# Attention backward on one core: the q rows on ScalarE's queue, more dK blocks ahead of the reciprocal, and an earlier start of V's work in the last turn

## The chip, the core and the metric

The kernel runs on one of the eight cores of a Trainium2 chip. A core has five engines with queues of their own: TensorE (PE, whose weight loads are listed as PEld), VectorE (DVE), ScalarE (ACT), GpSimd (POOL) and SyncE (SP). Sixteen DMA engines move data between HBM and SBUF; here nearly all transfers are issued from SP's queue, in order. An instruction waits on semaphores until what it needs is there, and whatever stands behind it on its queue waits with it. The metric is the device time in microseconds. Before the change it is 634.97 us (median of three runs, 634.79 to 635.12).

## The reference

There are 32 heads, one query row each (Sq = 1), 8192 keys and values of 128 numbers, all bf16. Forward output and three gradients are wanted:

```python
scores = einsum('bhqd,bhkd->bhqk', q, k) * 128 ** -0.5
attn = softmax(scores, axis=-1)
out = einsum('bhqk,bhkd->bhqd', attn, v)
# returned: out, dq, dk, dv for a given grad_out
```

With p the softmax row of a head and g its row of grad_out, dv is the outer product of p and g, dp = V g, ds = p (dp - sum(p dp)) / sqrt(128), dq = K^T ds and dk is the outer product of ds and q. K and V are 67 MB each. Each is read once, and dk and dv, of the same sizes, are written once: 268 MB in all.

## The kernel before

**Turns.** Two heads make one pair, and pair t is worked on in turn t, of 16 (HP = 16). A K or V tile of a pair is 4.19 MB, [128 partitions, 128 rows, 128 numbers]. K has three buffers, V two. The gradient overwrites its input in place: `outer(t, "p", r)` writes one eighth of dV over V, and `outer(t, "ds", r)` one eighth of dK over K (both L363, on DVE); `store` (L373, on SP) then sends the tile out. In turn t the kernel finishes pair t-1's dK ("old" work, called by `dk(a, b)` for blocks a to b-1, with the store behind the block that completes a part), computes the softmax and dV of pair t, and starts pair t+1's scores. A 17th pass of the loop does the last dK.

**Scores.** `k_block(t, c)`: DVE transposes an eighth of K (L197), PE multiplies it with the q columns (L205) into one PSUM bank. `s_back` transposes the result on DVE (L212), `s_top` and the head of `s_exp` find the maximum over the partitions with a PE transpose between (L217 to L227), ScalarE does the exponential (L230), and `s_sum` adds over partitions on PE (L235). `p_of` takes the reciprocal on DVE (L246), and ScalarE writes p four times (`p_rep`, L248) and puts it into a window (L241) for the contraction `contract(t, "p")` (PE, L341), which makes the forward output.

**V's part.** dP = V g wants V transposed. `v_bank(t, m)` transposes a sixteenth of it on PE, four matmuls into one of three PSUM tiles (L269), `v_copy` takes it to SBUF on ScalarE (L275); `v_part` is both. When four banks m = 4z to 4z+3 are copied, `v_scores(t, z)` multiplies them with grad_out's columns (PE, L286). In turns 3 to 14 (`wide(t)`, the loop's branch `blocks`) the second half of V goes by DVE transposes instead (`v_block`, L293, and `v_wide`, L303). Turns 0, 1, 2 and 15 have no such V blocks; turn 0 does all sixteen banks before the loop. `v_back` (L312, L315) transposes dP back on DVE, `ds_of` computes ds, `contract(t, "ds")` makes dq.

**Order.** It is written out by hand: within `tc.manual_schedule()` each engine runs its instructions in the order in which the program emits them. In turns 1, 2 and 15 that order is: dK blocks 0 to 2, banks 3 and 4, `s_back`, `s_top`, scores 0, banks 5 and 6, the exponential, banks 7 to 9 on PE, `s_sum`, copies 7 and 8, dK block 3, `p_of`, copy 9, scores 1, banks 10 and 11, the contraction, banks 12 and 13, scores 2, banks 14 and 15, scores 3, dK blocks 4 to 7, dV blocks 0 and 1, `v_back`, dV block 2, `ds_of`, `contract(t, "ds")`, and dV blocks 3 to 7. Banks 0 to 2 of pairs 1, 2 and 15 are done in the turn before, beside the last three K blocks. A dV block may not start before the banks and the contraction that read its part of V.

**Transfers.** SP issues, in this order: the q rows (L90), V of pair 0 in quarters, K of pair 0 in quarters, K and V of pair 1 (L81), K of pair 2. grad_out's rows come from ScalarE's queue (L91). Later, each turn's end issues the load of K and V two pairs ahead. A load of V waits until the store of dV from the same buffer has landed. In turn 0 the spare third K buffer holds V's transposes, so the load of K for pair 2 waits until `v_scores(0, 3)` is done.

Of the kernel before, what the change touches and what calls it, by code (L numbers as in the profile page):

```python
# [1 line left out]

# [13 lines left out]
NB = 8  # L16
TB = 4
# [10 lines left out]
def kernel(  # L28
# [11 lines left out]
    nc = tc.nc  # L40
# [46 lines left out]
        load(v, Vt, t, parts)  # L87

    rows = consts.tile([H, 2, D], BF16)
    nc.sync.dma_start(rows[:, 0, :], q.rearrange("b h s d -> (b h s) d"))  # L90
    nc.scalar.dma_start(rows[:, 1, :], grad_out.rearrange("b h s d -> (b h s) d"))  # L91
    load_v(0, 4)
    load_k(0, 4)
# [317 lines left out]
    for t in range(HP + 1):  # L411
        o = t - 1
        now, old = t < HP, t > 0
        parts = 4 if o == HP - 1 else 2 if o == HP - 2 else 1

        def dk(a, b):
            for r in range(a, b if old else a):
                outer(o, "ds", r)
                if (r + 1) % (NB // parts) == 0:
                    store(o, "ds", parts, r * parts // NB)  # L420

        blocks = now and wide(t)

        if blocks:

            dk(0, 5)
            s_back(t)
            s_top(t)
            for m in range(3):
                v_bank(t, m)  # L430
            v_block(t, 0)
            rs = s_exp(t)
            for m in range(3):
                v_copy(t, m)
# [12 lines left out]
            v_part(t, 7)  # L447
            v_block(t, 3)
            contract(t, "p")
            v_scores(t, 1)  # L450
            v_wide(t, 2)
            v_wide(t, 3)
            weights_do(t + 1)
            if wide(t + 1):
                weights_wide(t + 1)
        else:
            dk(0, 3)
            if now:
                if old:
                    v_part(t, 3)  # L460
                    v_part(t, 4)
                s_back(t)
                s_top(t)
                if old:
                    v_scores(t, 0)
                    v_part(t, 5)
                    v_part(t, 6)
                rs = s_exp(t)
                if old:
                    for m in (7, 8, 9):  # L470
                        v_bank(t, m)
                s_sum(t, rs)
                if old:
                    v_copy(t, 7)
                    v_copy(t, 8)
            dk(3, 4)
            if now:
                p_of(t)
                if old:
                    v_copy(t, 9)  # L480
                    v_scores(t, 1)
                    v_part(t, 10)
                    v_part(t, 11)
                contract(t, "p")
                if old:
                    v_part(t, 12)
                    v_part(t, 13)
                    v_scores(t, 2)
                    v_part(t, 14)
                    v_part(t, 15)  # L490
                    v_scores(t, 3)
                if t + 1 < HP:
                    if old:
                        weights_do(t + 1)
                    if wide(t + 1):
                        weights_wide(t + 1)
        if not now:
            dk(4, NB - 1)
            results()
            dk(NB - 1, NB)  # L500
            break
        dk(6 if blocks else 4, NB)
        fine = t == 0 or t == HP - 1
        outer(t, "p", 0)
        outer(t, "p", 1)
        if fine:
            store(t, "p", 4, 0)
        v_back(t)
        pd_sum(t)
        if t % ST == 0 and old:  # L510
            gather(o, "ds")
        outer(t, "p", 2)
        ds_of(t)
        contract(t, "ds")
        if t % ST == ST - 1:
            gather(t, "p")
        if t + 1 < HP:
            prepare(t + 1)
        else:
            gather(t, "ds")  # L520
        for r in range(3, NB):
            outer(t, "p", r)
            if fine and r % 2:
                store(t, "p", 4, r // 2)
            if t + 1 < HP and t != 1 and r >= HALF - 1:
                k_block(t + 1, r - HALF + 1)
        if not fine:
            store(t, "p")
        if t == 1:
            for c in range(HALF + 1):  # L530
                k_block(t + 1, c)
        if t + 1 < HP:
            for c in range(HALF + 1, NB):
                k_block(t + 1, c)
                if not wide(t + 1):
                    v_part(t + 1, c - HALF - 1)
            if t + 2 < HP:
                weights_q(t + 2)
        if 0 < t and t + 2 < HP:
            load_k(t + 2)  # L540
        if t + 2 < HP:
            load_v(t + 2, 4 if t == 0 else 1)
# [32 lines left out]
```

## Time and profile before

| what | value |
|---|---|
| median of three runs | 634.97 us |
| profiled execution: its own time, its span | 635.36 us, 633.57 us |
| DVE, PE, ScalarE busy | 558.9, 428.7, 158.0 us |
| HBM read, written | 134.23, 134.23 MB |
| mean granted TensorE clock | 0.833 |
| SP's waits ahead of a store for dV blocks, for dK blocks | 268.6, 72.0 us |
| SP's waits ahead of a load for the landing of a dV store, a dK store | 134.0, 100.4 us |

The span runs from the first to the last instruction; some 1.8 us lie around it. A row of a timeline gives start, duration, engine and line, output<-input, and in brackets the idle time of the engine before it and what ended it. In a group of issues the last column is the median time from issue to landing. A wait that is put down to one releaser can have had several.

### The profile page before, as it was taken

Reading aid. Unit: us, or ns where it says so; the run is one execution under the profiler, and the core shown is the slowest. Engines: PE = TensorE matmul, PEld = TensorE weight load, DVE = VectorE, ACT = ScalarE, POOL = GpSimd, SP = SyncE. Lnnn points to the kernel's source line nnn. Section 1 sums busy time; section 2 is a strip of 40 time slices with the busy share of each in tenths; the row PEclk is TensorE's granted clock in tenths of the full one; section 3 lists DMA queues with packets and bytes.
Section 4 is the critical chain, followed back from the end, with each engine's and each line's share of the span. In section 5 each row is a group of like instructions: output and inputs, shape, how many; then the busy total and the mean of one; then the engine's idle time right before and its main releaser. Section 6 shows DMA issues by size and latency. Waiting matters only on the chain.

```text
span 633.6 us, 7259 instructions
## 1 busy us (share of the span) xinstructions
PE 428.7 (68%) x2876; PEld 231.2 (36%) x2876; DVE 558.9 (88%) x662; ACT 158.0 (25%) x407; POOL 9.5 (1%) x27
## 2 busy tenths in 40 slices
PE   6767777766685765847766676765768658576860
PEld 5225335242341523315342332523425233152630
DVE  3788997999979899998998989899898899989793
ACT  6013416031230412204031130311303113040520
POOL 2000000000000000000000000000000000000000
PEclk9879888879789777798878798687986878887865
DMA  8999999999999999999999999999999999999997
GB/s 355 440 428 398 438 418 415 425 430 409 432 433 431 435 431 431 435 432 431 429 431 430 432 431 430 430 432 438 436 426 434 431 434 427 432 430 429 426 414 325
DMA packets 12177, 268.92 MB, mean 424 GB/s; under 512 B 1520, under 2 KB 1520, under 8 KB 1520
## 3 DMA queue, kind: packets, MB, share of 16 engines
q1 hardware_dynamic: 12096, 268.47, 99.2%
q8 instruction: 22, 0.36, 0.2%
q14 instruction: 11, 0.09, 0.0%
q10 hardware_dynamic: 48, 0.01, 0.0%
HBM read 134.23 MB, written 134.23 MB: 424 GB/s over the span
## 4 chain that ended last, share of the span: by engine, by line
DVE 38%; DMA 27%; PE 22%; issue 9%; ACT 2%; DVEq 0%; SPq 0%; ACTq 0%
DVE XK_sb L197 15%; DMA K<-in_k_dram 14%; DMA out_dram<-K 13%; DVE K L363 11%; PE T_ps L269 10%; DVE V L363 6%; PE dp_ps L303 5%; PE acc_p L341 3%; PE dp_ps L286 2%; ACT XV_sb L275 1%; DVE sT L212 1%; DVE dpT L312 1%; PE m_ps L220 1%; DMA V<-in_v_dram 1%; DVE ds_rep L331 1%
## 5 line engine op out<-in xcount | busy, mean ns | idle before, releaser
L205 PE MATMUL s_ps<-XK_sb,q_win 128*128 128x512 bf16 x512 | 148.6, 431 | 50.5 <-DVE XK_sb L197 48.3
L197 DVE STREAM_TRANSPOSE XK_sb<-K 128x1024 f32<-128x1024 f32 x128 | 152.2, 1221 | 3.5 <-DMA K<-in_k_dram 3.3
L363 DVE TENSOR_TENSOR V<-p_rep,qd 128x2048 bf16<-128x2048 bf16 x128 | 152.0, 1203 | 3.2 <-DMA K<-in_k_dram 2.0
L363 DVE TENSOR_TENSOR K<-ds_rep,qd 128x2048 bf16<-128x2048 bf16 x128 | 147.8, 1207 | 0.1
L269 PE MATMUL T_ps<-ident_f,V 128*128 128x128 f32 x640 | 108.1, 333 | 0.3 <-DMA V<-in_v_dram 0.2
L205 PEld LDWEIGHTS <-q_win 128*128 128x128 bf16 x512 | 53.4, 106 | 138.6 <-issue 102.7
L269 PEld LDWEIGHTS T_ps<-ident_f,V 128*128 128x128 f32 x640 | 97.5, 176 | 14.5 <-ACT XV_sb L275 1.6
L275 ACT COPY XV_sb<-T_ps 128x512 f32<-128x512 f32 x144 | 79.0, 586 | 78.7 <-PE T_ps L269 78.3
L293 DVE STREAM_TRANSPOSE XV_blk<-V 128x1024 f32<-128x1024 f32 x48 | 59.6, 1241 | 9.1 <-PE dp_ps L303 8.7
L341 PE MATMUL acc_ds<-K,win_ds 128*32 128x512 bf16 x512 | 47.8, 540 | 27.8 <-ACT win_ds L241 27.8
L220 PE MATMUL m_ps<-ident_f,top 128*128 128x128 f32 x16 | 6.2, 389 | 72.6 <-DVE top L219 72.6
L303 PE MATMUL dp_ps<-XV_blk,do_wide 128*128 128x512 bf16 x192 | 51.2, 399 | 0.0
L182 ACT COPY q_win<-q_blk 128x16 bf16<-128x16 bf16 x16 | 4.2, 260 | 156.7 <-PE s_ps L205 156.2
L341 PE MATMUL acc_p<-V,win_p 128*32 128x512 bf16 x512 | 32.1, 394 | 2.6 <-ACT win_p L241 2.4
L341 PEld LDWEIGHTS <-win_ds 128*32 128x32 bf16 x512 | 15.9, 122 | 48.1 <-ACT win_ds L241 27.2
L220 PEld LDWEIGHTS m_ps<-ident_f,top 128*128 128x128 f32 x16 | 2.6, 161 | 79.4 <-issue 71.4
L286 PE MATMUL dp_ps<-XV_sb,do_win 128*32 128x512 bf16 x288 | 24.3, 413 | 8.1 <-ACT XV_sb L275 8.1
L230 ACT ACTIVATE e<-sT,nbias 128x128 f32<-128x128 f32 x16 | 8.2, 515 | 80.8 <-DVE nbias L227 80.8
L303 PEld LDWEIGHTS <-do_wide 128*128 128x128 bf16 x192 | 17.3, 100 | 28.3 <-issue 14.3
L312 DVE STREAM_TRANSPOSE dpT<-dp_ps 128x512 f32<-128x512 f32 x16 | 11.5, 717 | 13.9 <-PE dp_ps L303 13.0
L341 PEld LDWEIGHTS <-win_p 128*32 128x32 bf16 x512 | 13.0, 99 | 16.3 <-issue 6.7
L321 PE MATMUL m_ps<-pd,same 128*128 128x1 f32 x32 | 6.1, 260 | 18.8 <-DVE m_ps L315 18.8
(68 smaller groups left out, 203.4 us busy)
## 6 DMA issues: line engine op xcount, KB each, us to landing
K<-in_k_dram SPq DMA_DIRECT2D x15, 4096.0 KB, 19.3
V<-in_v_dram SPq DMA_DIRECT2D x14, 4096.0 KB, 19.3
out_dram<-K SPq DMA_DIRECT2D x14, 4096.0 KB, 26.3
out_dram<-V SPq DMA_DIRECT2D x14, 4096.0 KB, 18.4
V<-in_v_dram SPq DMA_DIRECT2D x8, 1024.0 KB, 9.6
out_dram<-V SPq DMA_DIRECT2D x8, 1024.0 KB, 12.8
K<-in_k_dram SPq DMA_DIRECT2D x4, 1024.0 KB, 16.3
out_dram<-K SPq DMA_DIRECT2D x2, 2048.0 KB, 11.9
```

What stands on the lines that cost most here:

```text
L197: nc.vector.transpose(X[:], Kt[t][:, c * BN:(c + 1) * BN, :].rearrange("p n d -> p (n d)").bitcast(F32).rearrange("p (n w j) -> p n w j", ...
L205: nc.tensor.matmul(x["s"][:], lhsT=q_win[:, 2 * w + e2, SL - 1 - c:SL - 1 - c + P], rhs=cols[:, w, e2], start=(c == 0 and w == 0 and e2 == 0),
L220: nc.tensor.transpose(x["m"][:, 128:256], top[:].to_broadcast([P, P]), ident_f[:])
L230: nc.scalar.activation(e[:].rearrange("p (c n) -> p n c", c=NB), x["sT"][:, :, 0:NB], ACT.Exp, bias=nbias[:], scale=scale, accum_out=rs[:])
L269: nc.tensor.transpose(T_ps[:, j, :], words[:, at * P:(at + 1) * P], ident_f[:])
L275: nc.scalar.copy(x["XV", z][:, i * TB:(i + 1) * TB, :], x.pop(("T", m))[:])
L286: nc.tensor.matmul(x["dp"][b * QD:(b + 1) * QD, :], lhsT=do_win[:, b // 2, e2, at:at + QD], rhs=cols[:, e2, :, b * QD:(b + 1) * QD], start ...
L293: nc.vector.transpose(X[:], Vt[t][:].rearrange("p n d -> p (n d)").bitcast(F32).rearrange("p (m r w j) -> p m r w j", r=SL, w=NW, j=QD)[:, ...
L303: nc.tensor.matmul(st[t]["dp"][:], lhsT=do_wide[:, 2 * w + e2, at:at + P], rhs=cols[:, w, e2], start=False, stop=(r == SL // 2 - 1 and w = ...
L312: nc.vector.transpose(dpT[:].rearrange("p m r -> p (m r)"), x.pop("dp")[:])
L341: nc.tensor.matmul(acc[which][b * QD:(b + 1) * QD, :], lhsT=win[which][:, g, at:at + QD], rhs=X[:, 4 * g:4 * g + 4, :].rearrange("p n d -> ...
L363: nc.vector.tensor_tensor(X[:, a:b, :].rearrange("p n (a b) -> p n a b", b=R), x[which][:, a:b, :].unsqueeze(2).to_broadcast([P, BN, D // ...
```

## The change

Three things change.

The q rows are issued by ScalarE, ahead of grad_out's rows, and no longer by SP ahead of the first V load.

In turns without V blocks (1, 2 and 15), `dk(3, 6)` stands where `dk(3, 4)` stood: dK blocks 4 and 5 come before the reciprocal, and blocks 6 and 7 stay behind it. The banks are taken from a running list. In turns 1 and 2, two banks (5 and 6) are transposed before the exponential and copied after it; `s_sum` comes next, then bank 7 and scores 1; behind `p_of` banks 8 to 10, the contraction, and banks 11 to 15 with scores 2 and 3.

For turn 15, banks 0 and 1 are done in turn 14 beside K blocks 3 and 4, and banks 2 to 4 beside K blocks 5 to 7, so that turn 15 starts at bank 5: banks 5 and 6, scores 0, banks 7 and 8 before the exponential, copy 7, scores 1, copy 8, `s_sum`, bank 9; behind `p_of` banks 10 and 11, scores 2, bank 12, the contraction, banks 13 to 15, scores 3. In turn 15 four dV blocks instead of two come before `v_back`, with the first two quarter stores behind blocks 1 and 3.

The number of matmuls, transposes, blocks, copies and transfers is the same, and so is the order of SP's other transfers.

```diff
-    nc.sync.dma_start(rows[:, 0, :], q.rearrange("b h s d -> (b h s) d"))
+    nc.scalar.dma_start(rows[:, 0, :], q.rearrange("b h s d -> (b h s) d"))
...
         else:
+            done = 5 if t == HP - 1 else 3 if old else NV
+            rest = iter(range(done, NV))
+
+            def v_more(count):
+                for m in islice(rest, count):
+                    v_part(t, m)
+                    if (m + 1) % (NM // TB) == 0 and m + 1 > NM // TB:
+                        v_scores(t, m * TB // NM)
+
             dk(0, 3)
             if now:
-                if old:
-                    v_part(t, 3)
-                    v_part(t, 4)
+                v_more(1)
+                v_more(1)
                 s_back(t)
                 s_top(t)
                 if old:
                     v_scores(t, 0)
-                    v_part(t, 5)
-                    v_part(t, 6)
+                    ahead = list(islice(rest, 2))
+                    for m in ahead:
+                        v_bank(t, m)
                 rs = s_exp(t)
                 if old:
-                    for m in (7, 8, 9):
-                        v_bank(t, m)
+                    for m in ahead:
+                        v_copy(t, m)
+                        if (m + 1) % (NM // TB) == 0:
+                            v_scores(t, m * TB // NM)
                 s_sum(t, rs)
-                if old:
-                    v_copy(t, 7)
-                    v_copy(t, 8)
-            dk(3, 4)
+                v_more(1)
+            dk(3, 6)
             if now:
                 p_of(t)
-                if old:
-                    v_copy(t, 9)
-                    v_scores(t, 1)
-                    v_part(t, 10)
-                    v_part(t, 11)
+                v_more(3)
                 contract(t, "p")
-                if old:
-                    v_part(t, 12)
-                    v_part(t, 13)
-                    v_scores(t, 2)
-                    v_part(t, 14)
-                    v_part(t, 15)
-                    v_scores(t, 3)
+                v_more(NV)
...
-        dk(6 if blocks else 4, NB)
+        dk(6, NB)
         fine = t == 0 or t == HP - 1
-        outer(t, "p", 0)
-        outer(t, "p", 1)
-        if fine:
-            store(t, "p", 4, 0)
+        early = 4 if t == HP - 1 else 2
+        for r in range(early):
+            outer(t, "p", r)
+            if fine and r % 2:
+                store(t, "p", 4, r // 2)
         v_back(t)
         pd_sum(t)
...
-        outer(t, "p", 2)
+        outer(t, "p", early)
         ds_of(t)
...
-        for r in range(3, NB):
+        for r in range(early + 1, NB):
             outer(t, "p", r)
             if fine and r % 2:
                 store(t, "p", 4, r // 2)
             if t + 1 < HP and t != 1 and r >= HALF - 1:
                 k_block(t + 1, r - HALF + 1)
+                if t + 1 == HP - 1 and r >= NB - 2:
+                    v_part(t + 1, r - NB + 2)
...
-                    v_part(t + 1, c - HALF - 1)
+                    v_part(t + 1, c - HALF - 1 + (2 if t + 1 == HP - 1 else 0))
```

More of the change, by code (lines that the diff above doesn't have):

```diff
@@ L1 @@
 from contextlib import ExitStack
+from itertools import islice
 import concourse.bass as bass
@@ L497 @@
         if not now:
-            dk(4, NB - 1)
+            dk(6, NB - 1)
             results()
```

## The prediction

> **What bounds the kernel now.** I read the page's second and third parts first, because the kernel reads and writes 268 MB in 634 us and the first question is whether the transfers ever pause.
>
> ```profile
> DMA  8999999999999999999999999999999999999997
> GB/s 355 440 428 398 438 418 415 425 430 409 432 433 431 435 431 431 435 432 431 429 431 430 432 431 430 430 432 438 436 426 434 431 434 427 432 430 429 426 414 325
> ...
> q1 hardware_dynamic: 12096, 268.47, 99.2%
> q8 instruction: 22, 0.36, 0.2%
> ```
>
> SP's queue (q1) keeps all 16 DMA engines occupied for 99.2% of the span. Only the first and the last slice fall below nine tenths. Then I asked for the sums by stage; the last two columns are DMA share and GB/s, the one before them PE's granted clock:
>
> ```profile
> 57.00:165.00 108.00, 77.48 (x555) 42.37 (x553) 98.12 (x116) 32.43 (x81) 0.94 (x3) 0.84 1.01 425
> 165.00:555.00 390.00, 264.64 (x1710) 138.41 (x1710) 360.29 (x414) 88.48 (x240) 3.12 (x10) 0.84 1.00 431
> ...
> 602.00:604.00 2.00, 1.68 (x17) 1.07 (x17) 2.00 (x3) 1.50 (x4) 0.00 (x0) 1.00 0.86 356
> 604.00:628.00 24.00, 8.70 (x60) 5.26 (x59) 18.47 (x21) 3.05 (x10) 0.00 (x0) 0.56 1.00 421
> 628.00:634.00 6.00, 0.00 (x0) 0.00 (x0) 0.00 (x0) 0.00 (x0) 0.00 (x0) 0.50 0.33 139
> ```
>
> The engines pause once between the start and 628 us: at 602 to 604 the share is 0.86, so 2 x 0.14 = 0.28 us are lost. After 628 they run out one by one until about 632.7. The chain of waits speaks another language (its largest shares are DVE 38%, DMA 27%, PE 22%, and its last 9 us are DVE's dK blocks), but it follows instructions back, not the queue of transfers. So third, SP's issues in order of time, and for single issues the time from issue to landing (last column):
>
> ```profile
> 0.73 0.38 SPq L90 DMA_DIRECT2D rows<-in_q_dram  x1
> 1.17 2.02 SPq L81 DMA_DIRECT2D V<-in_v_dram  x4
> ...
> 104.16 0.34 SPq L373 DMA_DIRECT2D out_dram<-K  x1
> 120.03 0.34 SPq L373 DMA_DIRECT2D out_dram<-V  x1
> ```
>
> ```profile
> out_dram<-K SPq DMA_DIRECT2D x1, 4096.0 KB, 20.0
> out_dram<-V SPq DMA_DIRECT2D x1, 4096.0 KB, 13.8
> ...
> out_dram<-K SPq DMA_DIRECT2D x1, 1024.0 KB, 9.1
> ```
>
> The K store issued at 104.16 lands at 124.2, the V store issued at 120.03 at 133.8, 9.7 us apart: 4.19 MB at 431 GB/s is 9.7 us. The second store had waited in a full queue. The last store of all (issued 623.62, 9.1 us) lands at 632.7; the three K stores before it (616.15, 618.42, 620.69; 9.1, 9.3, 9.5) at 625.3, 627.7, 630.2. They are issued 2.27 us apart, DVE's pace for two blocks, but land 2.47 us apart: the transfers set the pace, and each waits some 6.5 us. A store could leave 5 us later and land at the same time.
>
> So the bound is first issue + bytes / rate + run-out. An edit counts if it moves the first large load, or starves the queue.
>
> **Part 1, q rows (L90).** Before, the first V load leaves SP at 1.17, behind the q load, which takes SP from 0.735 to 1.11. Without it the V load leaves at 0.735: 0.43 us sooner, on the path. Both issue queues start at 0.73, so nothing holds SP back. ScalarE issues q and then grad_out, 0.42 us later than now; its table load moves from 1.18 to about 1.6. q lands 1.6 us after issue now, grad_out 1.8 on ScalarE's queue, so q would come at 2.5 instead of 2.35, grad_out at 2.95 instead of 2.52. Beside the first V packets, which both precede now, they could take longer; no row shows that, so I bound it by 0 and by the 4.8 us that the first V quarter takes. Behind them: DVE's four copies (start 2.39), PE's columns, the V banks (start 5.98), the V scores that release the K load of turn 2 at 17.47. By then loads are queued until 44.0 (the V load issued at 8.42 lands after 35.6). Even 4.8 us late costs nothing; I take 0. Nothing else on SP's queue changes order. Gain 0.43, between 0 (the engines start no sooner for another reason) and 0.43.
>
> **Part 2, six dK blocks ahead of the reciprocal, turns 1 and 2.** In turn 1 the rows are:
>
> ```profile
> 59.76 3.80 PE L269 MATMUL T_ps<-ident_f,V 128*128 128x128 f32 x20
> 65.60 1.91 PE L341 MATMUL acc_p<-V,win_p 128*32 128x512 bf16 x32
> 70.83 0.62 PE L286 MATMUL dp_ps<-XV_sb,do_win 128*32 128x512 bf16 x8 [0.72 <-ACT XV_sb L275]
> 63.82 0.17 DVE L246 RECIPROCAL rinv<-m_ps 128x1 f32<-128x1 f32 x1 [2.72 <-PE m_ps L235]
> 71.49 0.72 DVE L312 STREAM_TRANSPOSE dpT<-dp_ps 128x512 f32<-128x512 f32 x1 [0.30 <-PE dp_ps L286]
> ```
>
> The 2.72 us wait goes: three dK blocks run 59.88 to 63.3 (1.14 each), and the row sum comes behind two banks, not five: 59.76 + 8 x 0.19 + 0.4 = 61.7. The reciprocal is at 63.3, 0.5 sooner. What is late next is PE. Nine banks follow the sum instead of six. Bank 7 (0.8, half clock), its copy (0.6) and the scores (0.7) take it to 63.8; three banks at 0.136 a matmul to 65.4; the contraction, 1.9, to 67.3, as now. But then bank 11 (0.55), its copy (0.6), scores (0.62) to 69.1; banks 12 to 15 (2.1) and the last copy to 71.9; scores to 72.5, where now they end at 71.45. DVE, done with dK at 66.1, waits for bank 12 (69.7) before it may overwrite V: 3.6 us idle, then the dV blocks to 72.0. The dP transpose starts at 72.5 instead of 71.49: 1.0 us later, and from there all is as now. Turn 2 has the same rows and adds another 1.0.
>
> Who waits: SP's V stores, at 80.3 and 120.03, would leave at 81.3 and 122.0. The K stores ahead of them land at 84.5 (68.95 + 15.6) and 124.2, 0.43 sooner by part 1. A new transfer needs some lead: the first V load's bytes begin to flow about 1.1 us after issue, and the 0.28 us loss at 602 would fit up to 2.0. With 1.1 the stores must leave by 83.0 and 122.6, with 2.0 by 82.1 and 121.7. Cost 0 to 0.3; I take 0, since a landing includes the end of the last engine and the others have queued work until shortly before. K's stores leave 2.9 us sooner, into the same queue: 0.
>
> At one place the Trainium skill bears on this. PE's clock was 0.5 from 60.6 to 64.0, after a pause of only 1.8 us (57.15 to 58.96), then 1.0 until 74.2. The Trainium skill's page "TensorE: Matmul & The Clock Gate" (section "HAM oscillation") gives as rule that PE should have no idle gap over about 3.4 us, or its clock is halved; by it my new gaps, 0.7 us at most, keep the full clock and the sum stands; the trace is stricter than that rule, which is why a halved clock is a rival below.
>
> **Part 3, the last turn.** Two V banks more stand in turn 14, ahead of the last K blocks. V of turn 15 lands at 564.48 + 19.3 = 583.8, just as PE is done with K block 3; the two banks (1.1) lie in PE's pauses before the score transpose at 591.1. Scores 1 now stand ahead of the row sum and wait for the copy after the exponential: sum at about 595.8, still before the third dK block ends (596.7). The reciprocal comes 0.6 sooner, the second half of K's store leaves at 599.5 instead of 602.47, the dP transpose at about 605.7 instead of 605.07 but with four dV blocks done rather than two. DVE ends 2 x 1.13 - 0.6 = 1.6 us sooner, at 621.3; the last store leaves about 1.9 us sooner. All of it goes into a queue that lags by 5 us: 0. The 0.28 us at 602 is refilled, but only in engines that had run ahead; those that end last had work. I take 0, bounds 0 and 0.28.
>
> **Sum.** The profiled execution took 635.36: span 633.57 and 1.8 around it; it stands 0.39 above the median of 634.97. 635.36 - 0.43 = 634.93; against the median 634.97 - 0.43 = 634.54, say 634.5. Unknown on top: 22 instruction packets share q8's 0.2%, about 0.9 us each on one engine of the 16. If the new order puts one more or less on the engine that ends last, the time moves by 0.9.
>
> **Rivals.**
> *Slower: V stores too late.* If PE runs the stretch behind the contraction at half clock, the contraction costs 3.41 us (turn 0's row, mostly at half clock) instead of 1.91, twenty bank matmuls 0.19 instead of 0.136, two groups of scores some 0.3 more each: 3.2 us a turn. In one turn: V store of turn 2 at 125.2, 2.6 after the point (122.6), 634.54 + 2.6 = 637.1; in both 128.4, 5.8 after it, 640.3. It decides (over 0.2%) once the two turns' delay exceeds 2.6 + 1.7 = 4.3 us. For: clock drops at 94.7 and 74.2. Against: PE is now no emptier there. 0.10.
> *Faster: the tail follows DVE.* If the last landing follows its issue, the 1.9 us come through: 632.6. For: the chain's last 9 us are DVE. Against: 2.47 us between landings. 0.10.
> *The q move does nothing* (start bounded elsewhere): 634.97. For: the first packets are slow, share 0.80 at 2 to 3 us. Against: it was SP's own issue that came first. 0.14.
>
> **How the numbers follow.** The forecast has 0.66. 0.2% (1.27 us) is about what a measurement of this kernel can tell from no change. Faster: 0.10 (tail) + 0.10 (forecast with one instruction packet less, 633.6) = 0.20. Slower: 0.10 + 0.04 (packet and starving together). Same: 0.66. Range: down by one packet, the 0.28 and the 0.39 between executions, 634.54 - 1.57 = 633.0; up by packet and 0.39 and 1 us of starving to 636.8. Outside are most of the tail rival and the late-store rival: under 0.2.
>
> **What would show it.** First V load on SP at 0.73 to 0.75; reciprocal's wait in turns 1 and 2 gone, the dP transpose about 1 us later; V stores near 81 and 122 with DMA share 1.0 behind them; last store near 621.7, landing near 632.2, so its time from issue to landing about 10.5 us instead of 9.1. A share below 0.95 between 80 and 130, or a V store after 122.6, would make it wrong upwards; landings closer than 2.4 us in the tail, downwards.

## The result and the profile after

The changed kernel takes 641.91 us (median; 640.51 to 643.87), the kernel before 634.91 on the same chip: ratio 1.0112, 95% interval 1.0082 to 1.0142, so 7.0 us slower where 634.5 was forecast. The profiled execution of after took 640.51, its span is 638.7. Line numbers are one higher than before (L363 is now L364, L373 is L374).

The page's second and third parts, of after:

```profile
DMA  8999989999999999999999999999999999999997
GB/s 362 438 437 392 437 345 438 375 427 389 437 436 430 434 428 429 434 429 434 430 429 430 436 432 429 426 431 430 434 436 428 431 429 436 432 431 434 423 418 307
...
q1 hardware_dynamic: 12048, 268.46, 98.7%
```

A slice is 16 us here. The sixth (80 to 96 us) has fallen from 418 to 345 GB/s, and the eighth (112 to 128) from 425 to 375. The sums by stage show it better; of after (the last three columns are PE's granted clock, DMA share, GB/s):

```profile
78.00:100.00 22.00, 17.99 (x108) 8.68 (x101) 20.66 (x23) 4.48 (x11) 0.00 (x0) 0.72 0.90 371
100.00:122.00 22.00, 14.65 (x140) 7.71 (x139) 17.99 (x23) 8.73 (x22) 0.31 (x1) 0.92 0.99 405
122.00:127.00 5.00, 2.44 (x11) 0.86 (x10) 5.00 (x6) 0.00 (x0) 0.00 (x0) 1.00 0.96 413
127.00:160.00 33.00, 23.25 (x159) 13.27 (x158) 30.54 (x37) 9.24 (x25) 0.31 (x1) 0.77 0.99 403
160.00:300.00 140.00, 97.42 (x638) 50.61 (x636) 132.17 (x151) 32.65 (x87) 1.25 (x4) 0.86 1.00 432
```

and the same stretches of before:

```profile
78.00:100.00 22.00, 17.03 (x102) 10.68 (x99) 18.41 (x23) 6.65 (x14) 0.00 (x0) 0.84 1.00 418
100.00:122.00 22.00, 15.32 (x126) 6.84 (x124) 21.59 (x24) 6.54 (x19) 0.31 (x1) 0.84 1.00 416
122.00:127.00 5.00, 3.32 (x14) 1.06 (x11) 5.00 (x6) 0.26 (x1) 0.00 (x0) 1.00 1.03 446
127.00:160.00 33.00, 21.98 (x162) 12.79 (x163) 30.96 (x38) 8.96 (x24) 0.31 (x1) 0.84 1.00 419
160.00:300.00 140.00, 95.74 (x624) 50.27 (x622) 129.43 (x152) 33.57 (x91) 1.25 (x4) 0.83 1.00 432
```

The bytes that were not moved, at 431 GB/s: 22 x 47 / 431 = 2.4 us, 22 x 11 / 431 = 0.6, 5 x 33 / 431 = 0.4, 33 x 16 / 431 = 1.2. That is 4.6 of the 5.1 us by which the spans differ, all of it between 78 and 160 us. Behind 160 both kernels run at the same rate, up to the run-out (the end, where the engines finish one by one), in which the engines stood idle 3.06 us on average instead of 2.48.

Part of this is idle time, part is slow packets. Counted over the packet records of the trace (idle: the mean over 16 engines of the time without a packet of 8 KB or more; slow: what packets took beyond their usual 309, 612 and 1213 ns for 8, 16 and 32 KB): after stood idle 3.07 us from 78 to 210 us against 0.07 before, and lost 4.53 us to slow packets from 78 to 300 us against 2.84. By the same count over the whole span the 5.1 us are 3.0 us more idle time from 78 to 210, 1.8 us more in slow packets and 0.6 us more idle time at the run-out, less 0.3 us of idle time saved at the start. The profiled execution is the shortest of the four of after, so what the others lost on top of it is not in this trace.

Where it comes from stands in SP's issues, of after:

```profile
0.74 2.03 SPq L82 DMA_DIRECT2D V<-in_v_dram  x4
...
19.31 0.33 SPq L82 DMA_DIRECT2D K<-in_k_dram  x1
38.73 13.53 SPq L374 DMA_DIRECT2D out_dram<-V  x4
...
83.22 0.34 SPq L374 DMA_DIRECT2D out_dram<-V  x1
...
124.59 0.34 SPq L374 DMA_DIRECT2D out_dram<-V  x1
```

and of before:

```profile
36.69 13.53 SPq L373 DMA_DIRECT2D out_dram<-V  x4
...
80.30 0.34 SPq L373 DMA_DIRECT2D out_dram<-V  x1
...
120.03 0.34 SPq L373 DMA_DIRECT2D out_dram<-V  x1
```

The first load leaves 0.43 us sooner, as forecast. But turn 0's V store leaves at 38.73 instead of 36.69, turn 1's at 83.22 instead of 80.30, turn 2's at 124.59 instead of 120.03 (and turn 3's at 163.02 instead of 157.70). The engines stand idle 2.29 us around 81 to 84 us and 0.77 around 124 to 125, each time around a late V store. The lag grows in two places: in the head (2.04 us) and in turns 1 and 2.

**The head.** The small loads by issue, and the first work of DVE and PE, of after:

```profile
rows<-in_q_dram ACTq DMA_DIRECT2D x1, 8.0 KB, 3.4
rows<-in_grad_out_dram ACTq DMA_DIRECT2D x1, 8.0 KB, 5.5
```

```profile
19.44 0.46 DVE L141 COPY do_four<-tp_q 64x64 bf16<-64x64 bf16 x2 [12.15 <-PE tp_q L139]
19.93 9.33 DVE L198 STREAM_TRANSPOSE XK_sb<-K 128x1024 f32<-128x1024 f32 x8
```

```profile
7.70 9.60 PE L270 MATMUL T_ps<-ident_f,V 128*128 128x128 f32 x64
...
19.15 0.26 PE L139 MATMUL tp_q<-ident,four 32*128 32x32 bf16 x4
```

and the same work of before, DVE, then PE:

```profile
17.61 0.46 DVE L140 COPY do_four<-tp_q 64x64 bf16<-64x64 bf16 x2 [10.47 <-PE tp_q L138]
```

```profile
5.98 7.38 PE L269 MATMUL T_ps<-ident_f,V 128*128 128x128 f32 x48
...
17.31 0.26 PE L138 MATMUL tp_q<-ident,four 32*128 32x32 bf16 x4
```

Both rows were issued as V's packets began to flow, and took 3.4 and 5.5 us instead of 1.6 and 1.8; grad_out's came at 6.65 us instead of 2.52. PE's V banks need them, and started at 7.70 instead of 5.98. DVE's copy `do_four`, which makes grad_out's columns for pair 1, waits for a PE transpose that stands behind all of turn 0's V banks and scores; it slipped from 17.61 to 19.44. DVE's K transposes come behind it, and so everything that DVE does in turn 0.

**Turn 1.** DVE's rows of after:

```profile
59.72 0.71 DVE L213 STREAM_TRANSPOSE sT<-s_ps 128x512 f32<-128x512 f32 x1
...
65.44 0.17 DVE L247 RECIPROCAL rinv<-m_ps 128x1 f32<-128x1 f32 x1
...
71.48 2.36 DVE L364 TENSOR_TENSOR V<-p_rep,qd 128x2048 bf16<-128x2048 bf16 x2 [3.20 <-issue]
74.41 0.72 DVE L313 STREAM_TRANSPOSE dpT<-dp_ps 128x512 f32<-128x512 f32 x1 [0.57 <-PE dp_ps L287]
```

The reciprocal's wait is gone, and DVE waits 3.20 us ahead of dV block 0 instead. From the score transpose to the dP transpose it takes 14.69 us. In before these were 57.69 and 71.49 us, 13.80 apart.

### The profile page after: what moved, and what is told of

Read it like the earlier page. It is cut to its first block, busy times and chain, and to the rows that moved or that the text cites. A ratio compares the mean times of both kernels' runs of the same rounds, so it can differ in the third digit from the quotient of the medians.

```text
span 638.7 us, 7256 instructions
## 1 busy us (share of the span) xinstructions
PE 424.8 (67%) x2876; PEld 225.5 (35%) x2876; DVE 558.3 (87%) x662; ACT 158.1 (25%) x407; POOL 9.3 (1%) x27
## 4 chain that ended last, share of the span: by engine, by line
DVE 34%; DMA 30%; PE 22%; issue 9%; ACT 3%; DVEq 0%; ACTq 0%; SPq 0%
DMA out_dram<-K 18%; DVE XK_sb L198 13%; DMA K<-in_k_dram 12%; DVE K L364 11%; PE T_ps L270 9%; DVE V L364 4%; PE dp_ps L304 4%; PE acc_p L342 3%; PE dp_ps L287 2%; PE s_ps L206 2%; ACT XV_sb L276 2%; DVE sT L213 1%; DVE dpT L313 1%; DMA rows<-in_grad_out_dram 1%; PE m_ps L221 1%
## 5 line engine op out<-in xcount | busy, mean ns | idle before, releaser
L206 PE MATMUL s_ps<-XK_sb,q_win 128*128 128x512 bf16 x512 | 150.4, 434 | 52.9 <-DVE XK_sb L198 50.6
L364 DVE TENSOR_TENSOR V<-p_rep,qd 128x2048 bf16<-128x2048 bf16 x128 | 152.1, 1203 | 11.6 <-issue 6.4
L364 DVE TENSOR_TENSOR K<-ds_rep,qd 128x2048 bf16<-128x2048 bf16 x128 | 147.8, 1207 | 0.1
L270 PE MATMUL T_ps<-ident_f,V 128*128 128x128 f32 x640 | 103.4, 322 | 0.7 <-DMA V<-in_v_dram 0.7
L270 PEld LDWEIGHTS T_ps<-ident_f,V 128*128 128x128 f32 x640 | 92.2, 169 | 15.0 <-issue 4.3
L304 PE MATMUL dp_ps<-XV_blk,do_wide 128*128 128x512 bf16 x192 | 49.1, 387 | 0.0
L342 PE MATMUL acc_p<-V,win_p 128*32 128x512 bf16 x512 | 33.9, 411 | 3.8 <-ACT win_p L242 3.8
L304 PEld LDWEIGHTS <-do_wide 128*128 128x128 bf16 x192 | 16.9, 98 | 27.1 <-issue 12.5
```

Source lines behind the costliest of these rows:

```text
L206: nc.tensor.matmul(x["s"][:], lhsT=q_win[:, 2 * w + e2, SL - 1 - c:SL - 1 - c + P], rhs=cols[:, w, e2], start=(c == 0 and w == 0 and e2 == 0),
L270: nc.tensor.transpose(T_ps[:, j, :], words[:, at * P:(at + 1) * P], ident_f[:])
L304: nc.tensor.matmul(st[t]["dp"][:], lhsT=do_wide[:, 2 * w + e2, at:at + P], rhs=cols[:, w, e2], start=False, stop=(r == SL // 2 - 1 and w = ...
L342: nc.tensor.matmul(acc[which][b * QD:(b + 1) * QD, :], lhsT=win[which][:, g, at:at + QD], rhs=X[:, 4 * g:4 * g + 4, :].rearrange("p n d -> ...
L364: nc.vector.tensor_tensor(X[:, a:b, :].rearrange("p n (a b) -> p n a b", b=R), x[which][:, a:b, :].unsqueeze(2).to_broadcast([P, BN, D // ...
```

## The experiments

Two theories stood at the outset (the texts on record give them letters of their own). One: the V stores leave too late, so whatever delays DVE's chain on its way to the stores of turns 1 and 2 costs time. The rival: the parts harm by themselves, the q rows through the transfers (small loads among the large), the order of the turns through PE, and the late stores only go with it. All kernels were timed in five rounds beside the kernel before (634.9 to 635.2). What they gave, with one profiled execution of each (sT to dpT: score transpose to dP transpose in turns 1 and 2; V stores: issues of turns 1, 2, 3, the first half where they are split; idle 78 to 210 us and slow 78 to 300 us as counted above). A profiled execution can be up to 1.4 us shorter than the median of its kernel (q_only, banks_only, after, after_cols), so its column of times and its columns of causes are not of one and the same execution:

| run | time, us | ratio [95%] | sT to dpT | V stores | idle | slow |
|---|---|---|---|---|---|---|
| before | 634.9 to 635.2 | | 13.80, 13.93 | 80.30, 120.03, 157.70 | 0.07 | 2.84 |
| after | 641.91 | 1.0112 [1.0082, 1.0142] | 14.69, 14.69 | 83.22, 124.59, 163.02 | 3.07 | 4.53 |
| q_only | 636.57 | 1.0022 [1.0013, 1.0030] | 12.51, 12.51 | 80.97, 119.98, 157.53 | 0.53 | 2.64 |
| without_q | 639.22 | 1.0066 [1.0053, 1.0078] | 16.49, 15.07 | 82.90, 123.86, 161.29 | 2.05 | 4.39 |
| turns_1_2 | 638.24 | 1.0058 [1.0042, 1.0074] | 14.68, 14.68 | 81.84, 122.27, 159.93 | 0.92 | 4.51 |
| last_turn | 635.21 | 0.9999 [0.9991, 1.0008] | 12.50, 13.92 | 79.75, 119.33, 156.99 | 0.05 | 2.27 |
| late_dve | 637.29 | 1.0032 [1.0022, 1.0042] | 12.51, 12.52 | 81.09, 120.21, 157.74 | 0.24 | 2.96 |
| swapped | 635.52 | 1.0003 [0.9994, 1.0012] | 12.50, 12.51 | 79.58, 118.49, 155.98 | 0.04 | 1.43 |
| q_cols | 635.46 | 1.0003 [0.9994, 1.0011] | 13.97, 12.51 | 80.71, 119.97, 157.63 | 0.41 | 3.13 |
| dk_six | 636.20 | 1.0018 [1.0010, 1.0027] | 13.98, 13.38 | 80.21, 120.27, 157.73 | 0.06 | 3.15 |
| banks_only | 637.66 | 1.0048 [1.0032, 1.0064] | 13.64, 13.64 | 80.91, 120.32, 160.07 | 0.16 | 4.06 |
| halves | 635.04 | 0.9996 [0.9987, 1.0005] | 13.98, 12.54 | 75.98, 110.74, 157.46 | 0.09 | 1.74 |
| after_halves | 639.30 | 1.0071 [1.0055, 1.0088] | 14.68, 14.68 | 78.22, 115.02, 162.47 | 2.21 | 4.14 |
| after_halves3 | 638.94 | 1.0069 [1.0049, 1.0090] | 14.69, 15.20 | 79.68, 116.14, 153.45 | 0.49 | 6.03 |
| after_cols | 639.62 | 1.0071 [1.0056, 1.0086] | 15.25, 14.67 | 81.73, 122.18, 159.85 | 1.14 | 4.51 |
| after_cols_halves | 638.16 | 1.0042 [1.0026, 1.0058] | 16.51, 15.07 | 78.44, 114.92, 161.39 | 1.37 | 4.71 |
| q_cols_halves | 634.59 | 0.9992 [0.9983, 1.0001] | 14.00, 12.54 | 76.17, 110.86, 157.58 | 0.05 | 1.93 |

### Which part: one part alone

**The q rows alone** (before, with the first line of the diff).

```diff
-    nc.sync.dma_start(rows[:, 0, :], q.rearrange("b h s d -> (b h s) d"))
+    nc.scalar.dma_start(rows[:, 0, :], q.rearrange("b h s d -> (b h s) d"))
```

> Only the q rows move to ScalarE's queue; all else as before. Theory H (head: q and grad_out now queue behind the V packets, grad_out lands 5.5 us after its issue instead of 1.8, DVE's chain is 2.0 us late from turn 0 on, and the V stores of turns 1 and 2 come too late for the transfer queue): V store of turn 1 at 82.3, of turn 2 at 122.1; in the changed kernel the first of them left at 83.2 and the engines lost 2.2 us, so at 82.3 they lose about 1.4 us less 0.3 from the earlier start: 636.0, up to 637 with slower packets. Theory B (the bank order of turns 1 and 2 alone does the harm): 634.5. Theory L (the last turn does it): 634.5.

**All but the q rows** (after, with that line put back).

> The changed kernel with the q rows back on SP. Theory H: rows land at 2.4 and 2.5 again, V store of turn 1 at 81.2 and of turn 2 at 121.8, both still before the queue runs dry: 634.9 to 635.4. Theory B or L: the harm stays, 640 to 642.

**The order of turns 1 and 2 alone** (before, with the new branch for `t < HP - 1` only).

> Only the new order of turns 1 and 2 (six dK blocks, banks from the list); q on SP, last turn as before. Theory H: dP transposes 0.9 us later in each of the two turns, V stores at 81.2 and 121.8, 634.9 to 635.4. Theory B: 639 to 642. Theory L: 634.9.

**The last turn alone** (before, with the new branch for `t == HP - 1` and the two banks more in turn 14).

> Only the new order of the last turn (banks earlier, four dV blocks ahead of the dP transpose, six dK blocks ahead of the reciprocal); q on SP, turns 1 and 2 as before. Theories H and B: the last store leaves about 1.9 us sooner but lands when the queue lets it, 634.6 to 634.9. Theory L: 640 to 642. A tail bound by DVE: 633.

Measured: +0.22%, +0.66%, +0.58% and nothing. So both the q rows and the order of turns 1 and 2 harm by themselves, and the last turn's part is nil. Theory H, by which the head alone does the harm, had 634.9 to 635.4 for without_q and turns_1_2 and is not enough; theory B had no change for q_only and is not enough either. Alone the two parts cost 1.4 and some 3.7 us, together 7.0. That is more than the sum, as one would expect if each makes the V store of turn 1 late and before stands right at the edge, but the intervals are too wide to show it.

Sorted by that store's issue, the runs with whole stores were idle from 78 to 100 us: issue at 79.6 to 80.3, 0.01 to 0.04 us; 80.7 to 81.1, 0.10 to 0.49; 81.73 and 81.84, 1.06 and 0.81; 82.90, 1.65; 83.22, 2.29. Idle time begins at about 80.6 us, and in the four latest each microsecond behind that point brought 0.65 to 0.94 us of it.

The order is closer still if the store is set against the K store ahead of it in the queue, which lands at a different time on each of the 16 engines. Taken over the V stores of turns 1 to 12 in all 17 profiled executions (the first half where a store is split), no store that was issued at least 1.37 us before the first engine had finished the K store had more than 0.01 us of idle time around it (from 6 us ahead of its issue to 9 us behind it). Issued 1.1 to 0.1 us before that, stores had 0.03 to 0.69 us; issued up to 1.03 us behind it, 0.80 to 1.60; issued 1.74 us behind it, 2.1 and 2.25 (turn 3 of after_halves and turn 1 of after). So the idle time goes with this lead, whether the q rows, the order of the banks, the added work on DVE in late_dve or the splitting of earlier stores had made the store late.

The profile of last_turn shows also what turn 1 is in the old order when PE keeps its full clock. DVE, then PE:

```profile
58.45 0.71 DVE L213 STREAM_TRANSPOSE sT<-s_ps 128x512 f32<-128x512 f32 x1
...
70.95 0.72 DVE L313 STREAM_TRANSPOSE dpT<-dp_ps 128x512 f32<-128x512 f32 x1 [0.40 <-PE dp_ps L287]
```

```profile
60.52 2.48 PE L270 MATMUL T_ps<-ident_f,V 128*128 128x128 f32 x20
62.83 0.30 PE L236 MATMUL m_ps<-rs,same 128*128 128x1 f32 x2
...
65.06 1.91 PE L342 MATMUL acc_p<-V,win_p 128*32 128x512 bf16 x32 [0.22 <-ACT win_p L242]
66.90 1.09 PE L270 MATMUL T_ps<-ident_f,V 128*128 128x128 f32 x8
67.92 0.62 PE L287 MATMUL dp_ps<-XV_sb,do_win 128*32 128x512 bf16 x8
```

The twenty bank matmuls take 2.48 us, where the profiled execution of before had 3.80 at half clock. Score transpose to dP transpose is 12.50 us, not 13.80. At equal clock the new order costs 14.69 - 12.50 = 2.2 us a turn, not 0.9. The clock also blurs the parts: in q_only, where it was full, the lag behind before is 1.97 us at the score transpose, but only 0.67 us at turn 1's V store; in without_q, where it was partly halved, the same stretch takes 16.49 us and not 14.69.

### How the q rows harm

**The delay alone** (before, with two more K transposes on DVE in turn 0, whose output nothing reads).

```diff
+        if t == 0:
+            for i in range(2):
+                late = xkpool.tile([P, BN, NW, QD], F32, tag="XK", name="late")
+                nc.vector.transpose(late[:], Kt[0][:, 0:BN, :]...)
         for r in range(3, NB):
```

> The kernel before with two more K transposes on DVE in turn 0 (2.4 us of work whose output nobody reads); nothing else moves. Theory Q (any lateness of DVE's chain ahead of the V store of turn 1 drains the transfer queue, whatever made it late): V store of turn 1 at 82.7, of turn 2 at 122.4; engines idle about 1.6 us near 82, which all counts, for 636.5 to 638. Theory M (idle time in engines that ran ahead costs nothing, and the loss comes from the changed bank order itself): no change, 634.9 to 635.4.

**q on ScalarE, grad_out on SP** (so that V's first load leaves as late as before).

```diff
-    nc.sync.dma_start(rows[:, 0, :], q...)
-    nc.scalar.dma_start(rows[:, 1, :], grad_out...)
+    nc.scalar.dma_start(rows[:, 0, :], q...)
+    nc.sync.dma_start(rows[:, 1, :], grad_out...)
```

> The kernel before with q on ScalarE's queue and grad_out on SP's ahead of the V loads: both small loads again start before any V packet. If the place behind V packets made the rows late, both land 1.6 to 1.8 us after issue and the time is that of before, 634.9 to 635.4. If ScalarE's queue itself is slow for the q rows, q lands late, the V banks start late and the time is about 636.5.

**q on ScalarE, and grad_out's columns behind the K blocks** (DVE no longer waits for PE's V banks before its K transposes).

```diff
-    nc.sync.dma_start(rows[:, 0, :], q...)
+    nc.scalar.dma_start(rows[:, 0, :], q...)
     ...
-    columns(1, do_four)
     for c in range(NB):
         k_block(0, c)
+    columns(1, do_four)
```

> Only the q rows on ScalarE's queue, and in turn 0 the K transposes emitted ahead of the columns of grad_out for the wide weights, so that DVE no longer waits for PE's V banks there. If the late rows do harm only through that wait of DVE, the V store of turn 1 leaves by 80.3 again, and what is left is the first V load's earlier start: 634.6 to 634.9 beside 635.2 for the kernel before. If lateness reaches the queue another way: 636 to 637.

**The same in after.**

> The changed kernel, with grad_out's columns moved behind turn 0's first K blocks, so that DVE does not wait for PE's late V banks. If the q rows harm the changed kernel only by DVE's chain in turn 0: 638.2-639.5, as the changed kernel with q on SyncE (639.22), turn 1's V store near 82.3 us less. If the two small loads harm by the transfers themselves: 641-642.

Measured: 637.29 by the delay alone, 635.52 with the rows swapped, 635.46 with the columns moved. In swapped the rows land 1.9 and 1.7 us after issue and nothing is lost. In q_cols they land about as late as in q_only (3.6 and 5.7 us; 3.8 and 5.9 there), V's load leaves at 0.74, but DVE's first score transpose comes at 28.49 instead of 30.68 (rows of q_cols and q_only), and the loss is gone:

```profile
28.49 0.72 DVE L212 STREAM_TRANSPOSE sT<-s_ps 128x512 f32<-128x512 f32 x1
```

```profile
30.68 0.72 DVE L212 STREAM_TRANSPOSE sT<-s_ps 128x512 f32<-128x512 f32 x1 [1.12 <-PE s_ps L205]
```

The gain of the sooner V load, for which q_cols had 634.6 to 634.9, does not show. In after the same edit gives 639.62 instead of 641.91, just above its range and about as much as putting the q rows back (639.22). So the late rows harm through DVE's chain; a harm through the transfers is not seen.

One thing fits less well. late_dve lost 2 us as expected, but not where it was expected. Its V store of turn 1 left at 81.09, not 82.7, since PE kept its full clock there (12.51 us instead of 13.80), and only 0.24 us were idle. Its profiled execution is 1.7 us longer than before's: by the count above 1.24 us of it are idle time at the run-out, about 0.4 us slow packets and 0.2 us idle time near 82 us. Why a delay in turn 0 shows up at the end of the kernel is open.

### How the order of turns 1 and 2 harms

**Six dK blocks ahead of the reciprocal, banks as before.**

```diff
-            dk(3, 4)
+            dk(3, 6 if 0 < t < HP - 1 else 4)
...
-        dk(6 if blocks else 4, NB)
+        dk(4 if t == HP - 1 else 6, NB)
```

> Turns 1 and 2 with six dK blocks ahead of the reciprocal but the old order of the banks. If the bank order is what delays the dP transpose, this one has it where it was, 12.5 to 13.9 us after the score transpose: 634.9 to 635.4. If the later reciprocal delays it: 14.7 us and 637 to 638.5.

**The new order of the banks, dK blocks as before.**

> The kernel before, with only the new order of the V banks in turns 1 and 2; dK blocks 4 and 5 stay behind the reciprocal. Theory B (the order of the banks delays the V stores): 637.4-639, like the run that had the whole new order of turns 1 and 2 (638.24), score transpose to dP transpose 14.4-15.0 us, turn 1's V store at 81.3-82.2 us. Theory D (the dK blocks moved ahead are what costs): 635-636.2, as the run with six dK blocks alone (636.20), the V store by 80.6 us.

Each makes up about half of the longer chain. DVE's rows of banks_only, turn 1:

```profile
58.46 0.72 DVE L213 STREAM_TRANSPOSE sT<-s_ps 128x512 f32<-128x512 f32 x1
...
61.91 0.17 DVE L247 RECIPROCAL rinv<-m_ps 128x1 f32<-128x1 f32 x1
...
72.10 0.72 DVE L313 STREAM_TRANSPOSE dpT<-dp_ps 128x512 f32<-128x512 f32 x1 [0.57 <-PE dp_ps L287]
```

PE's rows of the same run behind the contraction:

```profile
64.92 1.91 PE L342 MATMUL acc_p<-V,win_p 128*32 128x512 bf16 x32
66.76 0.65 PE L270 MATMUL T_ps<-ident_f,V 128*128 128x128 f32 x4
68.09 0.62 PE L287 MATMUL dp_ps<-XV_sb,do_win 128*32 128x512 bf16 x8 [0.67 <-ACT XV_sb L276]
68.64 1.99 PE L270 MATMUL T_ps<-ident_f,V 128*128 128x128 f32 x16
71.44 0.62 PE L287 MATMUL dp_ps<-XV_sb,do_win 128*32 128x512 bf16 x8 [0.81 <-ACT XV_sb L276]
```

The contraction starts when it did in last_turn (6.46 and 6.61 us behind the score transpose). Behind it stand five banks instead of four, and a second wait for ScalarE's copy, 0.67 us: 13.64 instead of 12.50, 1.1 us. The dK blocks do the rest: in dk_six's turn 2, at full clock, the reciprocal comes 5.71 us behind the score transpose instead of 4.73, and the dP transpose at 13.38, 0.9 us later. 1.1 + 0.9 = 2.0 of the 2.2. In time, banks_only costs 0.48% and dk_six 0.18%, together 0.66%, against 0.58% for both at once. The time of banks_only lies in the range of its theory B, but its chain (13.64 us) and its V store (80.91) lie short of it, so neither of its theories holds alone; dk_six, at 636.20, lies between its two. So the longer chain is shown, but not how these two kernels lose some 3 and 1 us by it: their V stores left soon enough that 0.10 and 0.01 us were idle from 78 to 100. In the profiled executions the excess over before is slow packets for the most part in banks_only (1.0 of 1.3 us) and idle time at the run-out in dk_six (0.65 of 0.85 us); why is open.

### Does the late store cost, or the lag behind it?

If only the store is late, it can be split: four dV blocks are ready some 4.6 us sooner.

```diff
         for r in range(early + 1, NB):
             outer(t, "p", r)
+            if t in (1, 2) and r % 4 == 3:
+                store(t, "p", 2, r // 4)
...
-        if not fine:
+        if not fine and t not in (1, 2):
             store(t, "p")
```

**Halves in after.**

> The changed kernel, with the dV stores of turns 1 and 2 in two halves of 2 MB, the first behind dV block 3. Theory Q (the queue's engines run dry from about 80.6 us on because turn 1's V store leaves too late): the first half leaves four dV blocks sooner, near 78.6 instead of 83.2 us, and near 120 instead of 124.6; the 2.29 us and 0.77 us that the engines stood idle behind 80 and 124 us go to under 0.3 each, and the time falls from 641.9 to 636-639, with the PE order and the dP transposes as late as before. Theory P (the new order of banks costs time of itself, through PE, and the late store only goes with it): 641-642, as without halves.

**Halves in before**, and **halves with q_cols**, as candidates for a kernel that beats both.

> The kernel before, with only the dV stores of turns 1 and 2 in two halves. If the kernel before stands right at the edge where its turn 1 store starts to cost (80.3 against 80.6 us), there is next to nothing to gain: 634.6-635.2. If the pauses of 0.7-1 us that nearly all engines show between 91 and 153 us (2.46 us of slow packets in 78-180 us) come from late V stores, they shrink and the time goes to 633.5-634.5.

> The q rows issued by ScalarE, grad_out's columns behind the first K blocks so that DVE's chain is not held up, and the dV stores of turns 1 and 2 in halves. The sooner first load (about 0.25 us) should show here if nothing downstream eats it: 634.7-635.0 against 635.2. If the two waiting small loads cost as much as the sooner V load brings: 635.2-635.6, as without halves (635.46).

In after_halves the first half leaves at 78.22, and the engines are busy at 80 us again. But the loss has moved to turn 3. SP's issues and two stretches of after_halves:

```profile
78.22 4.87 SPq L374 DMA_DIRECT2D out_dram<-V  x2
...
115.02 9.38 SPq L374 DMA_DIRECT2D out_dram<-V  x2
...
162.47 0.34 SPq L374 DMA_DIRECT2D out_dram<-V  x1
```

```profile
80.00:85.00 5.00, 2.30 (x17) 0.63 (x6) 5.00 (x6) 0.37 (x1) 0.00 (x0) 0.50 0.94 403
...
159.00:164.00 5.00, 4.70 (x17) 1.83 (x16) 4.75 (x5) 0.00 (x0) 0.00 (x0) 0.77 0.58 249
```

Turn 3's store is whole and 4.8 us later than before, and the queue, not held up earlier, runs dry ahead of it: 2.1 of 5 us are lost there. 639.30 instead of 641.91 is just above what theory Q had (636 to 639), and well below theory P (641 to 642): the late store costs, but most of its cost came back later. So a new pair: the lag of DVE's chain is paid wherever it meets a store with less in hand (L), or each late store costs by itself (S).

**Halves in turns 1, 2 and 3** (`t in (1, 2, 3)`).

> The changed kernel with the dV stores of turns 1, 2 and 3 in halves. With halves in turns 1 and 2 the engines no longer stood idle behind 80 and 124 us, but 2.19 us behind 160 us, where turn 3's V store left at 162.47 instead of 157.70. Theory L (a lag of DVE's chain of some 4.8 us is what costs; it is paid at the first store that has less in hand): turn 3's first half leaves near 154, the idle time at 160 goes, and turn 4's store, 3.6 us late, pays 1.5-2.2 us behind 199 us instead; 638-639.5, little better than 639.3. Theory S (single late stores cost, each by itself): the idle time goes and does not come back, 636.5-637.3.

**Halves in turns 1 and 2, and grad_out's columns moved**, which takes 2 us of the lag away at its source.

> The changed kernel with both: grad_out's columns behind the first K blocks, and the dV stores of turns 1 and 2 in halves. Theory L: DVE's chain lags by 2.6-3.2 us instead of 4.8; turn 3's store leaves near 160.5, when the queue is just about to run dry (near 160), idle time there 0.2-0.8 us; 636-637.3. Theory S: both late stores are split, 635-635.6.

With three turns split the time stays, 638.94, as L said (638 to 639.5). The idle time at 160 goes, but turn 4's store leaves at 200.59 instead of 197.28. The stretch of after_halves3 ahead of it:

```profile
199.00:203.00 4.00, 2.17 (x9) 0.86 (x9) 4.00 (x5) 0.00 (x0) 0.00 (x0) 1.00 0.99 414
```

Only 0.4 us are idle there, less than L said, but slow packets cost 6.03 us from 78 to 300 instead of 4.14: after_halves and after_halves3 lose 14.4 and 14.5 us to idle time and slow packets over the whole span. It looks as if a late store is paid in either form; no run here separates the two. after_cols_halves came out at 638.16, above both expectations. Its PE ran turn 1 at half clock (16.51 us), so that its turn 3 store left at 161.39, not 160.5, and 1.37 us were idle.

No kernel beats before: q_cols_halves, with V's load sooner, DVE's chain on time and the stores split, is at 0.9992 [0.9983, 1.0001], which a measurement of this kernel can't tell from no change. halves alone took 635.04, as it should if before stands just at the edge (634.6 to 635.2). The gain to 633.5 that fewer slow packets were to bring did not come: they fell from 2.46 to 0.70 us in 78 to 180, but 1.0 us of them came between 160 and 210, where before had 0.13.

## Why the prediction was wrong

Two steps failed: "Even 4.8 us late costs nothing; I take 0" in part 1, and "Cost 0 to 0.3; I take 0" in part 2, which rests on the point from which a late V store costs.

**The bound was right, the lead was not.** "First issue + bytes / rate + run-out" holds as an account: what the engines did not move from 78 to 160 us is nearly all of the difference. But I read slack off the tail, where stores wait 6.5 us in the queue, and off single landings, and did not list for every turn how long SP's queue lasts ahead of each V store. Turn 1 of before had next to none to spare.

**Part 1 failed at "Even 4.8 us late costs nothing".** The loads were queued until 44.0, and the K load of turn 2, 1.84 us late, did cost nothing (in q_cols it left at 19.92, 2.45 us late, and no time was lost). But I followed only who waits on SP. Behind the same V banks stands DVE's copy `do_four`, and behind that all of DVE's turn 0, then its turn 1. In before those 10.47 us of idle time ahead of the copy were plain in DVE's timeline. Of the 4.8 us taken as the upper bound of the rows' delay, 1.8 and 4.1 came (landings at 4.13 and 6.65 instead of 2.35 and 2.52), and 2.04 us of it reached turn 0's V store. The gain of 0.43 us was mis-sized too. V's first load left 0.43 us sooner and landed at 5.68 instead of 5.93 in after, but in the eight profiled executions in which it left at 0.73 or 0.74 it landed anywhere from 5.49 to 6.18; the mean idle time of the engines ahead of 57 us fell by 0.3 us in after, and the times of q_cols and q_cols_halves show no gain clear of noise. The Trainium skill's page "DMA: Bandwidth & Descriptors" (section "Issuing engines are not separate DMA queues") says that issuing from several engines saves only the time that the issuing takes on the sequencer. The runs agree: the sequencer's 0.43 us were saved, and the rows paid for it.

**Part 2 had the chain right and its price wrong.** The reciprocal's wait went, DVE idled 3.20 us ahead of dV block 0 (3.6 forecast), and the dP transpose came 14.69 us behind the score transpose (14.8 forecast). Against before's profiled execution the chain is 0.89 and 0.76 us longer in turns 1 and 2, close to the 1.0 that was forecast. That is luck in part: the forecast set a new order mostly at full clock against rows of before at half clock, and at equal clock the price is 2.2. What failed is "Cost 0 to 0.3; I take 0": turns_1_2 alone, whose V stores left at 81.84 and 122.27, close to the forecast 81.3 and 122.0, took some 3.7 us more. In after, with the head's lag, turn 1's store was 2.92 us late (2.04 + 0.89), turn 2's 4.56: another 0.76 in that turn, and 0.9 between, mostly because PE ran the K blocks nearer to half clock (granted 0.57 from 80 to 92 us, 0.86 in before) and DVE waited for it.

**The point from which lateness costs was wrong.** I put it at 83.0 and 122.6, from the last landing of the K store less 1.1 us, and took 0 beyond the forecast since "the others have queued work until shortly before". They had not: K's store landed first at 81.48 on one engine and last at 84.26 on another. The engine that ends first has nothing queued behind it, and a store that leaves after about 80.6 comes too late for it. So the lead of about 1.1 us was the right size (idle time began between 1.37 and 0.92 us), but it counts back from the first engine's landing, and I counted it from the last, 2.8 us later. At the end of the kernel the engines are spread no less (5.06 us from first to last landing of the last store; 3.98 before), which fits that what an early engine loses is not won back; the records do not tell the engines apart, so this was only argued. Both signs of being wrong upwards came: a DMA share of 0.90 from 78 to 100 us, and a V store at 124.59.

**Part 3 was right in its price, wrong in its rows.** last_turn changes the time by nothing. The dP transpose did not come at +0.6 but 3.6 us later (608.62 against 605.07, with four dV blocks done), since the four dV blocks waited 2.76 and 1.15 us for V's banks, and the last store left 0.85 us later, at 624.47; yet it landed at 632.69 against 632.68, 8.2 us instead of 9.1 after issue. The last landing follows the queue and not its own issue, so the rival that let the tail follow DVE is excluded.

**The rival that came** is "V stores too late", by a chance of 0.10. I had made it hang on a half clock behind the contraction; in the profiled execution PE had its full clock there. The two things that I had priced at nothing sufficed. Half clocks come on top: from 14.69 to 16.5 us in without_q and after_cols_halves, which would be one reason why executions of after differ by over 3 us and those of before by at most 2; that was only argued.

## What to carry to other kernels

Where a queue of transfers bounds the time, list for each store how long the queue lasts on the engine that runs dry first, and follow a delay along every engine that stands behind it, not only to the next issue. A lag of the engine that feeds the stores was not cured here by issuing parts of them sooner: it was paid at the next store with nothing in hand. Compare an order of work only with rows at the same granted clock.

## What the runs showed of the hardware

- **A small load behind large ones is slow.** 8 KB issued just as the 1 MB quarters began took 3.2 to 5.9 us to land instead of 1.6 to 1.9. The Trainium skill's page "DMA: Bandwidth & Descriptors" (section "Queues, rings and completion order") says that a DMA engine takes turns between its queues, a whole packet at a time. The late landings fit that, though no run here shows the size of such a turn.
- **PE's clock depends on where the chain falls.** The same instructions of turn 1, in the old order, take 12.5 us or 13.8 to 14.0, by whether PE keeps its full clock between the score transpose and the row sum. In before (granted 0.57 from 60 to 64 us) it was halved after a pause of 1.8 us; in last_turn a pause of 1.81 us at the same place left it full. In all 17 profiled executions, in either order, the clock was halved for a part of that stretch where turn 1's score transpose came at 57.93 us or sooner (eight executions, mean granted clock 0.67 to 0.76 over the 7 us behind it), and full where it came at 58.28 or later (nine). In turn 2 no such point divides them; why is open.
- **Slow packets come in bursts.** In 78 to 200 us, the 16 engines lose some 0.5 to 0.8 us on average in slow packets at certain times (91 to 94, 110 to 112 and 151 to 153 us in before). With late V stores there are more: in after at 94 to 96, 113 to 115, 135 to 137 and 154 to 157. With the stores of turns 1 and 2 split in before they are nearly gone there (0.70 us in 78 to 180 instead of 2.46). In halves some of them came later instead (1.0 us from 160 to 210). So they go with late stores for a part, and what an engine waits for in such a pause is open.
